# Turning x in 32x32 blocks on VectorE and moving it by transfers, with the token MLP two units later

## The chip, the core and the metric

The kernel runs on one core of one Trainium2 chip. A core has a matrix engine (TensorE), a vector engine (VectorE), an activation engine (ScalarE), a general engine (GpSimd) and a queue engine (SyncE), and 16 DMA engines that move data. Each engine runs its own list of instructions in order and waits on semaphores for the others. The metric is the time of one execution on the device, in microseconds (us); of several runs the median counts.

## The reference: what is computed

An attention with a threshold (only scores within tau of the row's maximum count) is followed by an MLP mixer: a token MLP, which mixes over the sequence, and a channel MLP. There are 8 batch rows, 8 heads, 576 tokens, 64 values a head; all of it is float32.

```python
def _attn_ref(q, k, v, tau):                                   # (8, 8, 576, 64)
    scale = 1.0 / np.sqrt(q.shape[-1])
    scores = scale * np.matmul(q, k.transpose(0, 1, 3, 2))
    thresh = np.max(scores, axis=-1, keepdims=True) - tau
    scores = np.where(scores >= thresh, scores, -1000000000.0)
    scores = scores - np.max(scores, axis=-1, keepdims=True)
    attn = np.exp(scores)
    attn = attn / (np.sum(attn, axis=-1, keepdims=True) + 1e-09)
    return np.matmul(attn, v)

def _moe_ref(x, w_tok1, w_tok2, w_ch1, w_ch2):                 # x: (8, 576, 512)
    xt = x.transpose(0, 2, 1)
    h = np.maximum(xt @ w_tok1, 0.0) @ w_tok2                  # 576 -> 256 -> 576
    u = x + h.transpose(0, 2, 1)
    h2 = np.maximum(u @ w_ch1, 0.0) @ w_ch2                    # 512 -> 1536 -> 512
    return u + h2
```

## The kernel before

The attention is cut into 144 units. A unit is up to 128 queries of two heads, eight or sixteen score matmuls; nine units make two pairs of heads (a half row), 18 make a batch row. In this text rows are counted from 0, as in the code. The unit of the nine whose t is 4 is shared between the two pairs of heads. From row 1 on the weights are turned on VectorE in 32x32 blocks, and 16 transfers per three units put the blocks in their places. SyncE issues them:

```python
    def turn_blocks(u):
        ...
        T = Ts[key]
        nc.vector.transpose(
            out=T[:, :, place, :].rearrange("p a (c x) -> p c a x", c=NK), in_=e.rearrange("p (c a x) -> p c a x", c=NK, a=4)
        )
        if place == GU - 1:                    # GU = 3: the last of three units
            ...
            for a in range(4):
                for i in range(4):
                    nc.sync.dma_start(out=eT[32 * a : 32 * a + 32, :, i, :], in_=T[32 * i : 32 * i + 32, a, :, :])
```

Two units later the values (attention times v) are computed from eT. They come out as x transposed, xT: columns of the model on the partitions, tokens along the row. The token MLP needs x with the tokens on the partitions, so TensorE turns it, and ScalarE copies the result to x_sb:

```python
    def token_mlp(b):
        xT = xTs.pop(b)
        ...
        def turn_x(t):
            M = MT[t]
            ps = ps_tr.tile([P, MAIN], F32, tag="tr", ...).rearrange("p (c x) -> p c x", c=NP)
            for p in range(NP):
                nc.tensor.transpose(out=ps[0:M, p, :], in_=xT[:, p, o + t * P : o + t * P + M], identity=ident)
            nc.scalar.copy(out=x_sb[0:M, t, :], in_=ps[0:M].rearrange("q p d -> q (p d)"))

        def tok1(m):
            ...
            for t in range(NT):
                nc.tensor.matmul(ps, lhsT=w1[:, t, P * m : P * m + P], rhs=x_sb[:, t, :], start=(t == 0), stop=(t == NT - 1))
            nc.scalar.activation(out=s["a"][:, m, :], in_=ps, func=AF.Relu)

        def tok2(c, f):
            ...                                # two matmuls, then xT += result on VectorE

        steps = [(0.44, lambda t=t: turn_x(t)) for t in range(NT)]        # 5 steps of 4 turns
        steps += [(4.3, lambda m=m: tok1(m)) for m in range(NTK)]         # 2 steps
        steps += [(0.97, lambda c=c, f=f: tok2(c, f)) for c in range(NCC) for f in range(2)]   # 8 steps
        return steps
```

The MLP is a list of such steps (the channel MLP gives the others), each with an estimate of its cost. The kernel puts them between the parts of the attention units, a quota in each unit, so that TensorE always has something to do. When the last values of a row are there, its token MLP is put into the list, alternating with old steps of the channel MLP:

```python
    def push(b):
        ...
        for i, step in enumerate(steps):
            n = 2 if i in (NT, NT + NTK) else 1
            todo.extend(old[:n] + [step])
            del old[:n]
        ...
        quota = (sum(c for c, _ in todo) - (KEEP if b else KEEP_FIRST)) / (UB - 1)
```

The end of a unit: ScalarE issues the loads of q and k in most units, and the values that are due are computed last.

```python
        if b_now:
            fill(0.4)
        if back and in_blocks(wb):
            turn_blocks(w)                     # w = u - 2
        ...
        if on:
            weigh(u)                           # the exponentials, with steps of the list between them
        ...
            if t in when:
                ...
                load_qk(n + m, (nc.scalar if b_now else nc.sync,) * 2, range(lo, hi))
        ...
        if due and in_blocks(due[0][1]):
            values_due(u)
```

Of the kernel before, what the change touches and what calls it, by code (L numbers as in the profile page):

```python
# [9 lines left out]
F32 = mybir.dt.float32  # L10
# [3 lines left out]
AF = mybir.ActivationFunctionType  # L14
# [3 lines left out]
P = 128  # L18
# [3 lines left out]
def kernel(  # L22
# [25 lines left out]
    nc = tc.nc  # L48
    B, H, S, D = q.shape
# [7 lines left out]
    NT = NI + 1  # L57
    MT = [P] * NI + [LAST]
    NP = H // 2
    NTK = DTOK // P  # L60
    NCC = DM // P
# [6 lines left out]
    const = ctx.enter_context(tc.tile_pool(name="const", bufs=1))  # L68
    ld = ctx.enter_context(tc.tile_pool(name="ld", bufs=2))
    work = ctx.enter_context(tc.tile_pool(name="work", bufs=2))  # L70
    small = ctx.enter_context(tc.tile_pool(name="small", bufs=6))
    ps_sc = ctx.enter_context(tc.tile_pool(name="ps_sc", bufs=2, space=bass.MemoryType.PSUM))
    ps_tr = ctx.enter_context(tc.tile_pool(name="ps_tr", bufs=2, space=bass.MemoryType.PSUM))

# [9 lines left out]
    units = [(b, 2 * w, t) for b in range(B) for w in range(NP // 2) for t in range(9)]  # L84
# [44 lines left out]
    x_sb = const.tile([P, NT, DM], F32, name="x_sb")  # L129
# [93 lines left out]
    def weight(n):  # L223

        nonlocal steps_done
        for k in range(steps_done, min(steps_done + n, 3 * len(pieces) + 1)):
            i, part = divmod(k, 3)
            if part == 0:
                on_gpsimd(i - 1)
                if i:  # L230
                    load_piece(i - 1 + NRAW)
            else:
                on_scalar(i + 1, part - 1)
            on_vector(i, part)
            steps_done = k + 1

    def weight_to(x):

        weight(max(int(x) - steps_done, 0))

    def need(i):

        weight(3 * i + 4 - steps_done)
# [28 lines left out]
    xTs = {}  # L272
# [3 lines left out]
    def in_blocks(b):  # L276
        return b > 0

    def prep(n):
        lq, lk = loaded.pop(n)  # L280
        made = []
        for src, name in ((lq, "qT"), (lk, "kT")):
            sb = work.tile([P, S], F32, tag=name, name=f"{name}_{n}")
            nc.vector.transpose(out=sb, in_=src.rearrange("p n d -> p (n d)"))  # L284
            made.append(sb)
        heads[n] = made
# [41 lines left out]
    def norm(u):  # L328
        e, rs = st[u]
        rr = small.tile([P, 2], F32, tag="rr", name=f"rr_{u}")  # L330
        nc.vector.tensor_scalar(out=rr, in0=rs, scalar1=1e-9, scalar2=None, op0=ALU.add)
        nc.vector.reciprocal(out=rr, in_=rr)  # L332
        for h in range(2):
            eh = e[:, S * h : S * h + S]
            nc.gpsimd.tensor_scalar(out=eh, in0=eh, scalar1=rr[:, h : h + 1], scalar2=1.0, op0=ALU.mult, op1=ALU.mult)  # L335
        st[u] = e
# [39 lines left out]
    def split_middle(n):  # L376

        lv, vl = vals[n], vlast[n % VL]
        for h in range(2):
            r = slice(D * h, D * h + D)  # L380
            nc.gpsimd.tensor_copy(out=vl[r, r], in_=lv[r, NI, :])
        vals[n] = lv, vl
# [37 lines left out]
                copies.append(lambda x=x, ps=ps: nc.vector.tensor_copy(out=x, in_=ps))  # L420


    def token_mlp(b):
        xT = xTs.pop(b)
        o = S * (b % 2)
        s = {}

        def turn_x(t):
            M = MT[t]
            ps = ps_tr.tile([P, MAIN], F32, tag="tr", name=f"tx_{b}_{t}").rearrange("p (c x) -> p c x", c=NP)  # L430
            for p in range(NP):
                nc.tensor.transpose(out=ps[0:M, p, :], in_=xT[:, p, o + t * P : o + t * P + M], identity=ident)  # L432
            nc.scalar.copy(out=x_sb[0:M, t, :], in_=ps[0:M].rearrange("q p d -> q (p d)"))

        def tok1(m):
            need(2)
            if m == 0:
                s["a"] = work.tile([P, NTK, DM], F32, tag="a", bufs=1, name=f"a_{b}")
            ps = ps_mm.tile([P, DM], F32, tag="mm", name=f"t1_{b}_{m}")
            for t in range(NT):  # L440
                nc.tensor.matmul(ps, lhsT=w1[:, t, P * m : P * m + P], rhs=x_sb[:, t, :], start=(t == 0), stop=(t == NT - 1))  # L441
            nc.scalar.activation(out=s["a"][:, m, :], in_=ps, func=AF.Relu)

        def tok2(c, f):
            need(6)
            ps = ps_mm.tile([P, HS], F32, tag="mm", name=f"t2_{b}_{c}_{f}")
            for m in range(NTK):
                nc.tensor.matmul(  # L448
                    ps, lhsT=s["a"][:, m, P * c : P * c + P], rhs=w2[:, m, HS * f : HS * f + HS], start=(m == 0), stop=(m == NTK - 1)
                )  # L450
            u = xT[:, c, o + HS * f : o + HS * f + HS]
            nc.vector.tensor_add(out=u, in0=u, in1=ps)  # L452

        steps = [(0.44, lambda t=t: turn_x(t)) for t in range(NT)]
        steps += [(4.3, lambda m=m: tok1(m)) for m in range(NTK)]
        steps += [(0.97, lambda c=c, f=f: tok2(c, f)) for c in range(NCC) for f in range(2)]
        return steps
# [49 lines left out]
    def fill(share):  # L507
        nonlocal credit
        credit += share * quota
        while todo and credit > 0:  # L510
            cost, step = todo.popleft()
            credit -= cost
            step()
        if not todo:
            credit = 0.0

    def push(b):
        nonlocal quota
        uT = xTs[b]
        steps, old = token_mlp(b), list(todo)  # L520
        todo.clear()

        for i, step in enumerate(steps):
            n = 2 if i in (NT, NT + NTK) else 1
            todo.extend(old[:n] + [step])
            del old[:n]
        todo.extend(old)
        for i in range(2) if b % 2 == 0 else range(2, (2 * S + GR - 1) // GR):
            todo.extend(channel_mlp(b - b % 2, uT, i))
        quota = (sum(c for c, _ in todo) - (KEEP if b else KEEP_FIRST)) / (UB - 1)  # L530
# [3 lines left out]
    b_now = 0  # L534
    LAG = 2

    def values_due(u):
        while due and due[0][0] <= u:
            _, b, p0, g = due.popleft()
            values(b, p0, g)  # L540
            if p0 == NP - 2 and g == 2:
                if not in_blocks(b):
                    return True
                push(b)
        return False

    for u in range(len(units) + LAG + 4):
        on = u < len(units)
        if u == UB:
            late.close()  # L550
            ps_mm = ctx.enter_context(tc.tile_pool(name="ps_mm", bufs=2, space=bass.MemoryType.PSUM))
        if on:
            b_now, p0, t = units[u]
            n = b_now * NP + p0
        w = u - LAG
        back = 0 <= w < len(units)
        if on:
            scores(u)

        last = False  # L560
        if due and not in_blocks(due[0][1]):
            last = values_due(u)
        if 0 < u <= len(units):
            norm(u - 1)
        if b_now:
            weight(2)
        else:

            weight_to(2.25 * (u - 1.5))
        while copies:  # L570
            copies.popleft()()
        if last:
            push(0)
        if back:
            wb, wp, wt = units[w]
            if not in_blocks(wb):
                for i in range(3):
                    turn(w, i)
            if wt % GU == GU - 1:
                g = wt // GU  # L580
                if g < 2:
                    split_middle(wb * NP + wp + g)
                due.append((u + (2 if in_blocks(wb) else 1), wb, wp, g))
# [3 lines that stand above are left out]
            turn_blocks(w)  # L587
        if b_now:
            weight(2)
        if on:  # L590
            weigh(u)
        elif b_now:
            fill(0.6)
        if b_now:
            weight(2)
        elif u == 0:
            on_scalar(0, 0)
            on_scalar(0, 1)
        else:
            weight_to(2.25 * (u - 1))  # L600
        if on:


            when = {3: (2, 0, 2), 4: (2, 2, 4), 5: (2, 4, 6), 6: (2, 6, 8), 8: (3, 0, 3), 0: (1, 3, 6), 1: (1, 6, 8)}
            if u == 0:
                load_qk(1, (nc.sync, nc.sync), range(0, 3))
            if t in when:
                m, lo, hi = when[t]
                if n + m < len(pairs):
                    load_qk(n + m, (nc.scalar if b_now else nc.sync,) * 2, range(lo, hi))  # L610
            if t in (3, 7) and n + 2 + t // 4 < len(pairs):
                load_v(n + 2 + t // 4)
            if t == 2:
                prep(n + 1)
            if t == 7 and n + 2 < len(pairs):
                prep(n + 2)
        if due and in_blocks(due[0][1]):
            values_due(u)
    need(len(pieces) - 1)
# [30 lines left out]
```

## Time and profile before

| what | before |
|---|---|
| time, median of three | 1379.77 us (1378.82 to 1380.43) |
| span of the profiled execution | 1375.1 us |
| mean granted clock of TensorE | 0.988 |
| the turns of x on TensorE (L432), 160 | 24.0 us busy |
| their copies on ScalarE (L433), 40 | 23.0 us busy, 583 ns each |
| the turns of weights on VectorE (L365), 126 | 172.1 us busy, 1366 ns each |
| the transfers of eT (L374), 672 | 108 KB each, 2.2 us from issue to landing |
| DMA queues of SyncE and ScalarE | 32.0% and 7.3% of the 16 engines' span |

An "L" with a number is a line of the kernel. In a group, "eT<-T" means that eT is written from T; xN counts instructions. "PE" is TensorE, "DVE" VectorE, "ACT" ScalarE, "POOL" GpSimd, "SPq" and "ACTq" the queue instructions of SyncE and ScalarE, among them the issues of transfers. Names: sc scores, e weights, T turned weights, eT moved weights, pv values, tx turned x, t the token MLP, c the channel MLP, g and a their activations. In the trace a float32 matmul of the program counts as two.

### The profile page before, as it was taken

To read this page: it belongs to the slowest core of one execution; us is meant where nothing else is said; L and a number is where in the kernel's file an instruction comes from. 1 tells how busy PE (TensorE), PEld (TensorE's weight loads), DVE (VectorE), ACT (ScalarE), POOL (GpSimd) and SP (SyncE) were. 2 spreads that over 40 slices of the span, in tenths; PEclk is the share of its full clock that TensorE was granted. 3 is DMA by queue.
4 is the path that set the end of the run, shared out by engine and by line. 5 is a ranking of instruction groups with operands and counts; after the bars stand their busy time and mean duration, and the time that the engine had idled before them with its cause. 6 is when DMAs were issued, how large, how long until landed. Compare 5 with 4: busy or idle time off the path is not lost.

```text
span 1375.1 us, 17691 instructions
## 1 busy us (share of the span) xinstructions
PE 1322.7 (96%) x6226; PEld 817.9 (59%) x6226; DVE 588.2 (43%) x1017; ACT 581.8 (42%) x1288; POOL 356.0 (26%) x683
## 2 busy tenths in 40 slices
PE   6877799999999999999999999999999999999998
PEld 3444465646565666565665567565656576575675
DVE  6788875445444443434244444434333453201000
ACT  5666654454445444443434444353333444120110
POOL 4555653222222222222122222222121222100000
PEclk9988999999999999999999999999999999999999
DMA  5434655454544354433344435434433442400000
GB/s 121 98 96 125 183 142 124 100 123 98 122 109 114 82 121 94 113 88 95 77 100 94 113 77 123 106 83 98 103 87 75 107 103 63 115 1 16 8 11 21
DMA packets 278871, 128.20 MB, mean 93 GB/s; under 512 B 200896, under 2 KB 271552, under 8 KB 278784
## 3 DMA queue, kind: packets, MB, share of 16 engines
q1 hardware_dynamic: 150176, 111.06, 32.0%
q10 hardware_dynamic: 128608, 16.01, 7.3%
q8 instruction: 50, 0.82, 0.3%
q14 instruction: 37, 0.30, 0.1%
HBM read 43.25 MB, written 9.44 MB: 38 GB/s over the span
## 4 chain that ended last, share of the span: by engine, by line
PE 85%; DVE 7%; DMA 2%; SPq 2%; ACT 1%; issue 1%; POOL 1%; ACTq 0%; DVEq 0%; POOLq 0%
PE c L486 26%; PE c L470 26%; PE sc L302 11%; PE pv L413 9%; PE t L441 5%; PE t L448 3%; PE pv L408 3%; DVE mx L307 2%; SPq L374 2%; PE tx L432 1%; PE c L482 1%; DMA eT<-T 1%; PE tr L353 1%; DVE wc L205 1%; ACT e L317 1%
## 5 line engine op out<-in xcount | busy, mean ns | idle before, releaser
L307 DVE TENSOR_REDUCE mx<-sc 128x1 f32<-128x576 f32 x288 | 204.5, 751 | 487.9 <-PE sc L302 487.5
L470 PE MATMUL c<-xT,wc 128*128 128x256 f32 (+1 forms) x1920 | 399.4, 362 | 2.1 <-DVE xT L452 1.2
L486 PE MATMUL c<-wc,g 128*128 128x512 f32 x864 | 390.5, 597 | 0.0
L470 PEld LDWEIGHTS c<-xT,wc 128*128 128x128 f32 x1920 | 334.5, 191 | 71.5 <-issue 27.6
L308 POOL TENSOR_SCALAR bias<-mx,toff 128x1 f32<-128x1 f32 x288 | 82.8, 288 | 799.3 <-DVE mx L307 742.3
L317 ACT ACTIVATE e<-sc,bias 128x576 f32<-128x576 f32 x288 | 199.6, 739 | 162.0 <-POOL bias L308 161.4
L486 PEld LDWEIGHTS c<-wc,g 128*128 128x128 f32 x864 | 157.8, 190 | 175.7 <-issue 174.0
L471 ACT ACTIVATE g<-c 128x256 f32<-128x256 f32 (+1 forms) x240 | 86.7, 362 | 334.1 <-PE c L470 317.9
L324 ACT ACTIVATE e<-e,ntau 128x576 f32<-128x576 f32 x288 | 220.7, 771 | 0.0
L335 POOL TENSOR_SCALAR e<-e,rr 128x576 f32<-128x576 f32 x288 | 215.6, 761 | 15.8 <-DVE rr L332 4.3
L302 PE MATMUL sc<-kT,qT 64*128 64x288 f32 (+1 forms) x1280 | 196.6, 447 | 11.1 <-DVE kT L284 7.1
L365 DVE STREAM_TRANSPOSE T<-e 128x1152 f32<-128x1152 f32 x126 | 172.1, 1366 | 6.3 <-DMA eT<-T 2.6
L302 PEld LDWEIGHTS sc<-kT,qT 64*128 64x128 f32 (+1 forms) x1280 | 107.4, 184 | 98.3 <-issue 59.1
L413 PE MATMUL pv<-eT,lv 128*64 128x384 f32 (+1 forms) x1024 | 136.8, 409 | 0.0
L413 PEld LDWEIGHTS pv<-eT,lv 128*64 128x64 f32 x1024 | 76.1, 138 | 51.0 <-issue 43.6
L491 DVE COPY o<-c 128x512 f32<-128x512 f32 x36 | 24.9, 692 | 177.5 <-PE c L486 177.5
L418 ACT COPY xT<-pv 128x384 f32<-128x384 f32 (+1 forms) x56 | 21.0, 401 | 157.5 <-PE pv L413 157.5
L448 PE MATMUL t<-w,a 128*128 128x288 f32 x256 | 75.2, 421 | 7.2 <-DVE xT L452 5.3
L441 PE MATMUL t<-x_sb,w 128*128 128x512 f32 x160 | 72.1, 598 | 0.0
L448 PEld LDWEIGHTS t<-w,a 128*128 128x128 f32 x256 | 45.6, 191 | 32.2 <-issue 11.4
L452 DVE TENSOR_TENSOR xT<-xT,t 128x288 f32<-128x288 f32 x64 | 28.2, 446 | 80.5 <-PE t L448 80.0
L324 ACT ACTIVATION_READ_ACCUMULATOR e<-e,ntau 128x1 f32 x288 | 56.5, 196 | 0.0
(44 smaller groups left out, 554.7 us busy)
## 6 DMA issues: line engine op xcount, KB each, us to landing
eT<-T SPq DMA_DIRECT2D x672, 108.0 KB, 2.2
scratch<-in_moe_w_ch_dram SPq DMA_DIRECT2D x24, 512.0 KB, 3.7
lv<-in_v_dram SPq DMA_DIRECT2D x32, 288.0 KB, 3.3
out_dram<-o SPq DMA_DIRECT2D x36, 256.0 KB, 2.2
lk<-in_k_dram ACTq DMA_DIRECT2D x111, 72.0 KB, 2.6
lq<-in_q_dram ACTq DMA_DIRECT2D x106, 72.0 KB, 2.3
lq<-in_q_dram SPq DMA_DIRECT2D x22, 72.0 KB, 3.2
lk<-in_k_dram SPq DMA_DIRECT2D x17, 72.0 KB, 3.3
```

Source lines behind the costliest of these rows:

```text
L302: nc.tensor.matmul(sc[h][rows, f, 0:HS], lhsT=qT[r, cols], rhs=kT[r, HS * f : HS * f + HS], start=True, stop=True)
L307: nc.vector.tensor_reduce(out=mx[:, c], in_=sc[h][:, :, 0:HS], axis=AX.XY, op=ALU.max)
L317: nc.scalar.activation(out=eh, in_=sc[h][:, :, 0:HS], func=AF.Prelu, bias=bias[:, h : h + 1], scale=SCALE, alpha=STEEP)
L324: nc.scalar.activation(out=eh, in_=eh, func=AF.Exp, bias=ntau, accum_out=rs[:, h : h + 1])
L335: nc.gpsimd.tensor_scalar(out=eh, in0=eh, scalar1=rr[:, h : h + 1], scalar2=1.0, op0=ALU.mult, op1=ALU.mult)
L365: nc.vector.transpose(out=T[:, :, place, :].rearrange("p a (c x) -> p c a x", c=NK), in_=e.rearrange("p (c a x) -> p c a x", c=NK, a=4))
L413: nc.tensor.matmul(to[r], lhsT=lv[:, j, :], rhs=e[j], start=False, stop=(c == NI - 1), skip_group_check=True)
L441: nc.tensor.matmul(ps, lhsT=w1[:, t, P * m : P * m + P], rhs=x_sb[:, t, :], start=(t == 0), stop=(t == NT - 1))
L448: nc.tensor.matmul(ps, lhsT=s["a"][:, m, P * c : P * c + P], rhs=w2[:, m, HS * f : HS * f + HS], start=(m == 0), stop=(m == NTK - 1))
L470: nc.tensor.matmul(ps, lhsT=wc1[:, j, c, :], rhs=uT[:, c, GR * i : GR * i + n], start=(c == 0), stop=(c == NCC - 1))
L471: nc.scalar.activation(out=s["g"][:, j, 0:n], in_=ps, func=AF.Relu)
L486: nc.tensor.matmul(flat, lhsT=s["g"][:, j, P * t : P * t + P], rhs=wc2[:, j, :], start=False, stop=(j == NJ - 1), skip_group_check=True)
```

## The change

From row 2 on x is no longer turned on TensorE. When the values of a half row are there, VectorE turns the half in 32x32 blocks within the next unit, and 16 transfers, half on SyncE and half on ScalarE, put the blocks in their places in x_sb, eight at the end of that unit and eight at the end of the one after. Then, two units later than before, the token MLP is put into the list; it has 10 steps in place of 15. The columns of x_sb stand in another order, so that one transfer moves runs of 64 elements; the activation after tok1 puts them back. The purpose is to free TensorE of the turns and ScalarE of their copies.

```diff
-    small = ctx.enter_context(tc.tile_pool(name="small", bufs=6))
+    small = ctx.enter_context(tc.tile_pool(name="small", bufs=5))
...
+    def x_in_blocks(b):
+        return b > 1
...
+    def turn_x_blocks(b, w):
+        xt = work.tile([P, S // 32 * 64], F32, tag="xt", bufs=1, name=f"xt_{b}_{w}")
+        o = S * (b % 2)
+        nc.vector.transpose(
+            out=xt.rearrange("q (c p d) -> q p c d", c=S // 32, p=2),
+            in_=xTs[b][:, 2 * w : 2 * w + 2, o : o + S].rearrange("q p (c r) -> q p c r", r=32),
+        )
+        return xt.rearrange("q (c x) -> q c x", x=64)
+
+    def move_x(b, w, xt, i):
+        if w == 0 and i == 0:
+            assert x_read[b - 1]
+        for a in range(4):
+            n = len(range(a, S // 32, 4))
+            eng = nc.scalar if a % 2 else nc.sync
+            eng.dma_start(
+                out=x_sb[32 * a : 32 * a + 32, 0:n, P * i + 64 * w : P * i + 64 * w + 64], in_=xt[32 * i : 32 * i + 32, a::4, :]
+            )
...
-            nc.scalar.copy(out=x_sb[0:M, t, :], in_=ps[0:M].rearrange("q p d -> q (p d)"))
+            nc.scalar.copy(out=x_columns(t, M), in_=ps[0:M].rearrange("q p (i d) -> q p i d", i=4))
...
-            nc.scalar.activation(out=s["a"][:, m, :], in_=ps, func=AF.Relu)
+            nc.scalar.activation(
+                out=s["a"][:, m, :].rearrange("q (c i d) -> q i c d", i=4, c=NCC),
+                in_=ps.rearrange("q (i c d) -> q i c d", i=4, c=NCC),
+                func=AF.Relu,
+            )
...
-        steps = [(0.44, lambda t=t: turn_x(t)) for t in range(NT)]
+        steps = [] if x_in_blocks(b) else [(0.44, lambda t=t: turn_x(t)) for t in range(NT)]
...
-            n = 2 if i in (NT, NT + NTK) else 1
+            n = 2 if len(steps) - i in (8, 10) else 1
...
-            if p0 == NP - 2 and g == 2:
+            if g == 2 and x_in_blocks(b):
+
+                moves.append((u, b, p0 // 2))
+            elif p0 == NP - 2 and g == 2:
...
-    for u in range(len(units) + LAG + 4):
+    for u in range(len(units) + LAG + 8):
...
+        if moves and u == moves[0][0] + 1:
+            xts = turn_x_blocks(*moves[0][1:])
...
+        if moves and u > moves[0][0]:
+            at, b, w = moves[0]
+            for i in range(2):
+                move_x(b, w, xts, 2 * (u - at - 1) + i)
+            if u == at + 2:
+                moves.pop()
+                if w:
+                    push(b)
```

The turn on VectorE stands after the maxima and sums of its unit and ahead of the unit's turn of weights; the moves stand after the unit's loads of q and k.

More of the change, by code (lines that the diff above doesn't have):

```diff
@@ L420, in values, with x_columns @@
                 copies.append(lambda x=x, ps=ps: nc.vector.tensor_copy(out=x, in_=ps))
+    x_read = {}
+    def x_in_blocks(b):
+        return b > 1
+    def x_columns(t, M):
+        return x_sb[0:M, t, :].rearrange("q (i p d) -> q p i d", i=4, p=NP)
+    def turn_x_blocks(b, w):
[15 more added lines that the diff above has]
+            )
     def token_mlp(b):
@@ L441, in tok1 @@
                 nc.tensor.matmul(ps, lhsT=w1[:, t, P * m : P * m + P], rhs=x_sb[:, t, :], start=(t == 0), stop=(t == NT - 1))
-            nc.scalar.activation(out=s["a"][:, m, :], in_=ps, func=AF.Relu)
+            nc.scalar.activation(
[3 more added lines that the diff above has]
+            )
+            x_read[b] = m == NTK - 1
         def tok2(c, f):
@@ L535 @@
     LAG = 2
+    moves = []
     def values_due(u):
```

## The prediction

> **What bounds the kernel now.** I read the page's summary and slices first, then the stretches of 100 us, the chain in order of time, the timeline of one unit, the waits. From the page (busy time of each engine; TensorE and its granted clock in 40 slices, in tenths):
>
> ```profile
> PE 1322.7 (96%) x6226; PEld 817.9 (59%) x6226; DVE 588.2 (43%) x1017; ACT 581.8 (42%) x1288; POOL 356.0 (26%) x683
> PE   6877799999999999999999999999999999999998
> PEclk9988999999999999999999999999999999999999
> ```
>
> From about 200 us on TensorE has nothing idle: the stretches view has it busy for 99.2, 97.8, 100.0, 100.0, 100.0, 100.0 us of the six hundreds from 200 to 800. VectorE and ScalarE are under half used there. The change acts only there (it begins with batch row 2, rows counted from 0), so what counts is TensorE time removed, and TensorE time newly spent waiting.
>
> The chain in order of time at row 2 (start, us, what) prices the removed turns:
>
> ```profile
> 428.89 0.44 PE tx L432 x4
> 429.32 2.58 PE c L486 x6
> 431.90 1.17 PE sc L302 x8
> 433.07 0.59 PE tx L432 x4
> ```
>
> A group of four turns takes 0.44 us, 0.59 us just after scores. The channel MLP too takes 2.77 us in place of 2.58 after scores, so that surplus goes to whatever comes next.
>
> The timeline of unit 58, which begins with the scores at 424.91, has what matters most, the SyncE queue:
>
> ```profile
> 427.78 1.36 DVE L365 STREAM_TRANSPOSE T<-e 128x1152 f32<-128x1152 f32 x1
> ...
> 429.21 10.29 SPq L374 DMA_DIRECT2D eT<-T  x16
> ```
>
> VectorE ends the turn of weights 4.2 us into the unit; then SyncE issues the 16 transfers of eT for 10.3 us, 0.60 us each and 0.04 between. The queue is full for more than a unit, though its engine computes nothing. Two lines of the waits (us in total, times, longest), the second from the queue's own list, show how near the edge this is:
>
> ```profile
> PE pv L408 <- DMA eT<-T: 3.3, 4, 1.6
> SPq L374 <- DMA lq<-in_q_dram: 51.8, 22, 4.8
> ```
>
> The first: TensorE already waits for eT now and then. The second: an eT transfer waits for a q load that ScalarE issues. No data ties the two. The built program counts the landing of all these transfers on eight counters, used in turn by both queues, and an issue waits until the counter's last user has landed.
>
> **What the Trainium skill says.** The page "VectorE: DVE Perf Modes", section "The three transpose paths": VectorE turns only 32x32 blocks within a bank, TensorE a whole 128x128 into PSUM. Hence the extra transfers here. Its times are for bf16; the trace's are used. "DMA: Bandwidth & Descriptors", section "Issuing engines are not separate DMA queues": transfers from all engines share the same DMA engines, and issuing from two only saves issue time, usually small. The trace disagrees on small: 10.29 us a burst. The same page, "Anatomy of one DMA — SWDGE (gpsimd) path", gives about 2 us of fixed cost for that path; eT on SyncE's queue lands 2.2 us after issue here. "TensorE: Matmul & The Clock Gate", section "Why this matters for your kernels": idle gaps over some 3 us between bursts halve the clock. The trace agrees: the clock is 0.91 in the two hundreds up to 200 us, where TensorE's timeline has gaps of 2 to 3.6 us (3.59 at 114.4), and 1.00 after.
>
> **The change part by part.**
>
> *Removed.* 30 groups of four turns (6 rows by 5). At row 2 they take 3 x 0.44 + 2 x 0.59 = 2.50 us, less 2 x 0.15 that passes on: 2.2 to 2.5 a row, **13 to 15 us** in all, every one of them on the path. Also 30 ScalarE copies of 583 ns, 17.5 us, beside other work: nothing.
>
> *Added on VectorE.* 12 turns of 128x1152, at 1366 ns (the weights' turn of the same size) 16.4 us, beside other work. But each stands ahead of the turn of weights in the unit after the values, so that unit's eT burst begins 1.4 us later: 5.7 us into the unit.
>
> *Added transfers.* 16 for each half row, half on each queue, eight in each of two units. In SyncE's order all eight of its moves come after the 16 of eT. At 0.35 to 0.6 us each (the range of SyncE's other issues in the trace: output 0.36, v 0.40 to 0.53, eT 0.60) with an output between, they take 4 to 5.5 us of queue.
>
> *Moved.* The token MLP stands two units later and two old steps ahead of its first matmul. I laid the changed kernel's TensorE order out with the durations of the chain (scores 1.17, 1.13 in the shared unit; two steps of second channel layer 5.35; one 2.77; a step of first layer 1.79, two after scores 3.65; values 3.38), from the start of the unit after the values:
> - rows 3 and 5: (1.13 + 5.35) + (1.17 + 2.77 + 1.79) + (1.17 + 3.65) = **17.0 us** until tok1.
> - row 2: 6.5 + 7.0 + 9.9 + 1.2 = 24.6 us; rows 4 and 6: 8.4 + 8.7 + 9.9 + 1.2 = 28.2 us. Values stand between here.
> - row 7: no scores are left and no burst stands in the way; 18 us for a chain of some 10.
>
> When is x there? Counters aside: 5.7 + 10.3 + 4 to 5.5 + 2.2 = 22 to 24 us. With the counters: in rows 3 and 5 the thirteenth eT issue waits for ScalarE's k load of the next unit to land, and the first and third moves of SyncE for ScalarE's own moves. Unit 59's second exponential ends 6.3 us after its scores in the trace; the next unit begins at 6.5, so 12.8, plus about 1 us because ScalarE itself waits for the landings of its q and k loads before two of its moves, load issues 0.8 and landing 2.5 (page: 2.6 for k): about 17. Four more eT issues, 2.6, then 5 of moves and output, then 2.2: about **26 us**. So tok1 of rows 3 and 5 waits between 5 (no counters) and 9 us; I take 7.5, **15 us for two**. A gap of that length also costs clock: one stretch of 3.4 us at half speed, as the clock record shows them in the first 200 us, 1.7 us each, **3 us**.
>
> The same counters push the end of eT itself in the eleven units that hold moves and a burst: the last issue ends at 18.9 to 19.6 us and lands 2.2 later, at 21 to 22 us (20 in unit 49, which is short). By the same laying out the values that need it come, in units 49, 58, 67, 85, 94, 103, 121, 130, 139, at 17.3, 19.9, 19.2, 24.2, 23.7, 21.1, 24.2, 23.7, 21.1 us (76 and 112 hold the waits of tok1 counted above). They fall short by some 2.7, 1.5, 2.5, 0, 0, 0.5, 0, 0, 0.5: **about 7 us at full; I take 4**, because today's waits for eT (3.3) fall partly at the same places.
>
> *No weight.* The columns of x stand in another order, which the activation after tok1 undoes by its output pattern; 16 activations of 597 ns on ScalarE, not on the path. Buffers of the small tiles go from six to five, which makes room for the turned x; none lives five units.
>
> Sum: -14 + 15 + 3 + 4 = +8. I shade it to +4, since every wait in it is an estimate that stacks the later of several times: **1384 us**.
>
> **Rivals.**
> 1. *Hidden transfers*: x arrives in time, only the removal counts: 1379.8 - 14 = 1366. For it: two units of extra delay were put in for just this, DMA engines are busy only 40 to 50% in the stretches, and rows 2, 4, 6, 7 come out in time. Against: SyncE's queue order in rows 3 and 5, which even without counters gives 22 us against 17.0.
> 2. *A wait takes the removal's place* (mine): 1375 if only the queue order counts (-14 + 2 x 5), 1388 with counters.
> 3. *ScalarE blocks*: its moves wait for eT transfers issued late in the burst, its exponentials slip, score buffers stay occupied, and TensorE waits for ScalarE in every moving unit: 11 x 2 to 4 us more, 1400 to 1420. Against: in the built order ScalarE's moves mostly wait for early ones of the burst or its own loads, and its engine is 42% busy.
> 4. *VectorE the bound*: 16.4 us on an engine used 40 of 100 us; worth nothing here.
>
> **Range and chances.** 2% is 27.6 us. Faster by that would take twice the removed turns: 0.02. Slower by that needs rival 3: 0.05. Within 2%: 0.93. The range that holds 8 in 10 goes from most of rival 1 (1367) to my sum with waits at full and some of rival 3: 1396.
>
> **What would show it.** TensorE: turns x160 become x40, busy less by 15 to 18 us; VectorE gains 12 turns of about 1.37 us. The waits get a new line, tok1 on the move of x, two long waits (5 to 10 us) in units 78 and 114 and none in rows 4, 6 and 7. The wait of values on eT grows from 3.3 to 6 to 12. SyncE's bursts of eT in moving units last 13 us or more. The clock dips after the two gaps. I am wrong if the tok1 wait is absent (then 1366), if it shows in even rows, or if TensorE waits for the weights' activation in ScalarE (rival 3).

## The result and the profile after

The changed kernel takes **1399.83 us** (median of 5 runs, 1399.02 to 1403.59) against 1379.77 before: 1.0147 times the time before, 95% interval 1.0127 to 1.0167. It is 20 us slower. The prediction was 1384.0 with a range of 1367 to 1396; the result lies above the range.

The page of the changed kernel, its summary and slices:

```profile
PE 1316.8 (94%) x6106; PEld 808.8 (58%) x6106; DVE 603.6 (43%) x1029; ACT 565.1 (40%) x1258; POOL 355.9 (25%) x683
PE   6877899999999999799999999979999999999998
PEclk8988999999999999999999999989999999999999
```

TensorE has 120 instructions less (6226 to 6106), but only 5.9 us less of busy time (1322.7 to 1316.8), and the span is 21.8 us longer. Past its first five slices the row of PE now has two 7s, the 17th slice (559 to 594 us) and the 27th. Up to the scores of unit 30 (211.28 us before, 213.35 after) TensorE has the same work; the traces of this text reach them at 210.9 to 216.8 us, so two traces can differ by some us there. From these scores to TensorE's last instruction it takes 1160.0 us before and 1179.7 after, and of this its idle time rises from 5.7 to 30.5 us. The waits of the changed kernel name it (us in total, times, longest):

```profile
PE t L471 <- DMA x_sb<-xt: 18.7, 3, 8.9
PE sc L302 <- ACT e L317: 9.2, 7, 2.0
PE pv L408 <- DMA eT<-T: 2.8, 3, 1.7
```

The first line is new: tok1 (tile t) waits for the transfers of x. The three waits are 8.89 us at 584.9 (unit 78, row 3), 8.56 us at 913.8 (unit 114, row 5) and 1.26 us at 1232.2 (row 7). Before, the second line read

```profile
PE sc L302 <- ACT e L317: 3.9, 4, 1.9
```

with all four waits in the first 200 us; now 3.96 us of the 9.2 lie after them. The wait of values for eT was 3.3 us and is not larger now.

The timeline of unit 76, whose scores stand in the chain at 567.89, shows how the first long wait arises (start, us, queue or engine, what, how many):

```profile
570.69 1.36 DVE L436 STREAM_TRANSPOSE xt<-xT 128x1152 f32<-128x1152 f32 x1
...
573.38 12.89 SPq L374 DMA_DIRECT2D eT<-T  x16
...
586.32 2.55 SPq L448 DMA_DIRECT2D x_sb<-xt  x4
588.98 0.53 SPq L527 DMA_DIRECT2D out_dram<-o  x1
589.55 2.54 SPq L448 DMA_DIRECT2D x_sb<-xt  x4
...
593.76 6.97 PE L471 MATMUL t<-x_sb,w 128*128 128x512 f32 x10 [8.89 <-DMA x_sb<-xt]
```

VectorE has x turned by 572.05, 4.2 us into the unit. SyncE takes up its eight moves only at 586.32, behind the 16 transfers of eT (12.89 us), and spends 5.77 us on them and an output. The last of them lands at 593.4, 25.5 us into the unit and 1.9 us after its own issue, so it is the issue that is late and not the transfer; the matmuls begin at 593.76. TensorE had reached tok1 at 584.87, 17.0 us into the unit.

The stretch ahead of the slow clock and the slow one (duration, then busy time of each engine, PEclk, share of DMA engines, GB/s):

```profile
578.00:588.40 10.40, 6.86 (x33) 4.98 (x31) 4.91 (x7) 4.84 (x12) 2.90 (x6) 1.00 0.64 151
588.40:598.60 10.20, 4.84 (x6) 2.19 (x7) 0.00 (x0) 0.00 (x0) 0.00 (x0) 0.50 0.16 48
```

The clock stands at 0.50 for 10.2 us. The first 5.4 us of it pass in the wait itself; the other 4.84 us are matmuls at half speed, which cost 2.4 us. The same happens once more at 916.1. The matmuls of tok1 take 66.0 us after 200 us in place of 61.4.

The chain of the changed kernel at row 2, where no tok1 waits, has a wait of the other kind:

```profile
452.29 4.50 PE t L471 x10
...
456.82 0.60 ACT a L472
457.42 0.64 ACT e L317
...
458.10 1.86 PE sc L302 x8
```

Before, a step of the channel MLP stood between the scores and tok1 there, and the scores behind tok1 did not wait:

```profile
451.58 2.77 PE c L486 x6
454.36 4.29 PE t L441 x10
458.65 1.17 PE sc L302 x8
```

In the changed kernel tok1 is the first step after the scores in this unit, and the only one. Its activation (a) stands ahead of the unit's exponentials (e) on ScalarE, and can't start before tok1 ends; so the exponentials start late, the score buffers come free late, and the next scores wait 1.32 us and then take 1.86 us in place of 1.17. That happens once in each of the rows 2, 4 and 6 (456.8, 778.1, 1106.2).

### The profile page after: what moved, and what is told of

It is laid out like the page before. It is cut to its first block, busy times and chain, and to the rows that moved or that the text cites. A ratio compares the mean times of both kernels' runs of the same rounds, so it can differ in the third digit from the quotient of the medians.

```text
span 1396.9 us, 17642 instructions
## 1 busy us (share of the span) xinstructions
PE 1316.8 (94%) x6106; PEld 808.8 (58%) x6106; DVE 603.6 (43%) x1029; ACT 565.1 (40%) x1258; POOL 355.9 (25%) x683
## 4 chain that ended last, share of the span: by engine, by line
PE 83%; DVE 7%; DMA 3%; SPq 2%; ACT 2%; issue 1%; POOL 1%; ACTq 0%; DVEq 0%; POOLq 0%
PE c L521 26%; PE c L505 25%; PE sc L302 11%; PE pv L413 8%; PE t L471 5%; PE t L483 4%; PE pv L408 3%; DVE mx L307 3%; SPq L374 2%; PE c L517 1%; DMA lk<-in_k_dram 1%; DVE wc L205 1%; ACT e L317 1%; PE tr L353 1%; DMA scratch<-in_moe_w_ch_dram 1%
## 5 line engine op out<-in xcount | busy, mean ns | idle before, releaser
L471 PE MATMUL t<-x_sb,w 128*128 128x512 f32 x160 | 76.5, 627 | 18.7 <-DMA x_sb<-xt 18.7
L471 PEld LDWEIGHTS t<-x_sb,w 128*128 128x128 f32 x160 | 31.3, 201 | 56.7 <-issue 54.4
```

## The experiments

All ratios are to the kernel before, run beside the experiment on the same chip. Line numbers shift by a few between variants. "Idle" means TensorE's idle time from the scores of unit 30 to its last instruction: 5.7 us before, 30.5 us in the changed kernel. "In the trace" times are of that same part, in one profiled execution each.

### Without the transfers of x

```diff
-            for i in range(2):
-                move_x(b, w, xts, 2 * (u - at - 1) + i)
```

From row 2 on, x_sb is not written any more, so the token MLP takes row 1's x in every later row. TensorE's order is that of the changed kernel.

> The changed kernel without its transfers of x (rows 2 to 7 then take row 1's x into the token MLP); every instruction of TensorE stands as in the changed kernel. My theory (the loss is waiting for the moved x, its clock cost and ScalarE held up by its moves): no wait of tok1 on the moves, no half clock after 200 us, so 1399.8 less 18.7 less 5 less 4, about 1372 us (1368 to 1377), that is the removed turns as a clear gain of some 8 us. Rival A (the new order of work, two units later and with ten steps, is what costs): TensorE's waits move elsewhere and it stays above 1390 us.

1375.22 us, 0.9963 (0.9953 to 0.9973). The group line of tok1:

```profile
L471 PE MATMUL t<-x_sb,w 128*128 128x512 f32 x160 | 71.8, 595 | 0.0
```

No wait, and no matmul at half clock. So the transfers cost 1399.83 - 1375.22 = 24.6 us (25.4 by the two ratios). But removing the turns and paying for no transfer saves only 5 us, and not the 14 us that the turns took (their busy time after 200 us falls from 16.7 to 2.6). Idle is 10.8 us, 5.2 more than before: scores 4.0 (0 before), channel MLP waiting for xT 2.2 (0.2), values 2.2 (2.4) and the second token layer 2.2 (2.8).

### The order alone, with the turns kept

```diff
-        steps = [] if x_in_blocks(b) else [(0.44, lambda t=t: turn_x(t)) for t in range(NT)]
+        steps = [(0.0 if x_in_blocks(b) else 0.44, lambda t=t: turn_x(t)) for t in range(NT)]
 ...
+            if x_in_blocks(b) and i < NT:
+                if i == 2:
+                    todo.append(old.pop(0))
+                todo.append(step)
+                continue
```

The turns and moves of x are taken out, and the turns on TensorE put back into the changed kernel's order, two and three groups around one old step.

> The changed kernel's order, but x turned by TensorE as before: the token MLP joins the list two units later, no turn by VectorE and no transfer of x, and the five groups of four turns of a row stand two and three around the old step ahead of its first matmul. Otherwise the order on TensorE is that of the changed kernel. Leaving the transfers out (turns gone, order changed) saved only 5 us of the 14 us of turns. My theory is that the order itself costs the rest: then this kernel, with turns and with that order, is 6 to 10 us slower than the kernel before: 1386 to 1390 us, with 1.3 us waits of scores for ScalarE in the even rows as in the changed kernel. The rival: the turns are worth only some 5 us because what they take comes back elsewhere, whatever the order; then it takes the time of the kernel before, 1379 to 1382 us.

1389.35 us, 1.0064 (1.0050 to 1.0078): 8.8 us slower than before, inside what the order theory expected; the rival falls. The chain of this kernel at row 2 has the same wait of scores behind tok1's activation:

```profile
451.55 4.50 PE t L471 x10
...
456.07 0.60 ACT a L472
456.67 0.64 ACT e L317
...
457.35 1.87 PE sc L302 x8
```

Idle is 12.5 us: scores 4.0, channel MLP waiting for xT 1.8, and 3.7 ahead of the turns themselves, which here stand close together and wait for ScalarE to empty their two buffers (0.2 before). Those 3.4 us more belong to how I placed the turns; the changed kernel does not have them. So by the medians the order accounts for 8.8 - 3.4 = 5.4 us of the 9 us missing from the turns' price.

The traces go further: 1160.0 us before, 1172.0 here, 1154.8 without the transfers. In the same order, then, leaving the turns out gives 17.2 us, 3.4 of them those waits and 13.8 the turns' own, which is their price in full. The order costs 12.0 - 3.4 = 8.6 us, and about 1.7 of these come from a stretch of 3.4 us at half clock (at 773.9) that the kernel without transfers does not have. In both kernels scores wait 4.0 us and are busy 1.9 us longer than before. So the order is most of the 9 us; whether it is all of it stays open.

### The transfers, three ways

**Token MLP three units later.**

```diff
-            if u == at + 2:
+            if u == at + 3:
                 moves.pop()
```

(The moves stay in the first two units.)

> The token MLP joins the list three units later in place of two, all else as in the changed kernel. My theory: x is there 25.9 us after the start of its moving unit, as in the trace, and tok1 of rows 3 and 5 now stands at 27 to 30 us: the two waits of 8.9 and 8.6 us and the two stretches at half clock vanish, the small waits of scores stay: 1375 to 1381 us. Rival A (lateness itself costs): later is worse, 1400 us or more. Rival B (DMA engines too slow for the moves): waits of tok1 shrink but stay, 1385 to 1395 us.

1376.24 us, 0.9967 (0.9954 to 0.9980). No tok1 wait; about 1 us from the kernel without transfers, though not in the same order: scores wait for ScalarE once and not three times, and values wait 4.8 us in place of 2.2. One unit more takes the moves out of tok1's way, not out of that of the values.

**The turn of x behind the turn of weights**, so that the burst of eT starts 1.4 us earlier:

```diff
-        if moves and u == moves[0][0] + 1:
-            xts = turn_x_blocks(*moves[0][1:])
 ...
             turn_blocks(w)
+        if moves and u == moves[0][0] + 1:
+            xts = turn_x_blocks(*moves[0][1:])
```

> VectorE turns x after its unit's weights, not ahead of them; TensorE's order is the same. The burst of eT then begins 1.3 us earlier. My theory: x still stands behind the whole burst, and the burst still waits for ScalarE's k load of the next unit, so tok1's waits shrink by 0 to 1.3 us each: 1397 to 1400 us. Rival C (the turn ahead of the weights is what makes x and eT late): the waits shrink by most of their length, below 1390 us.

1398.34 us, 1.0126 (1.0093 to 1.0158). The tok1 waits are 8.19, 8.09 and 1.26: shorter by 0.7 and 0.5. VectorE's turn counts on this path, for less than its length.

**ScalarE's moves all in the first unit, and its q and k loads in other units**, so that nothing of SyncE's burst waits for a load:

```diff
-            when = {3: (2, 0, 2), 4: (2, 2, 4), 5: (2, 4, 6), 6: (2, 6, 8), ...}
+            when = {3: (2, 0, 4), 6: (2, 4, 8), ...}
 ...
-            for i in range(2):
-                move_x(b, w, xts, 2 * (u - at - 1) + i)
+            first = u == at + 1
+            for i in range(4):
+                move_x(b, w, xts, i, ((1,) if first else ()) + ((0,) if first == (i < 2) else ()))
```

> ScalarE issues all eight of its moves at the end of the first unit and none in the second, and the four loads of q and k of the two moving units go to the units beside them, so that no eT transfer shares a counter with a later ScalarE transfer; SyncE's queue and TensorE's order are the same. My theory (the queue order is most of it, the counters some): the burst of eT falls from 12.9 to 10.3 us, and tok1 of rows 3 and 5 waits 6 to 7 us in place of 8.6 and 8.9: 1393 to 1397 us. Rival D (the shared counters are all of it): no wait, 1378 us. Rival E (counters have no part): burst and waits unchanged, 1400 us.

1401.97 us, 1.0145 (1.0115 to 1.0176): the time missed what was expected. The burst took 11.16 us (12.89 in the changed kernel, 10.3 expected) and the waits 6.96 and 7.18, close to what was expected; so of the 9 us the coupling of SyncE's issues to ScalarE's is worth 1.4 to 1.9, and most of the rest is queue. Waits of values rose from 3.2 to 4.0 and of scores from 4.0 to 4.6, and ScalarE's exponentials waited up to 5.3 us for landings of x. Idle fell by only 2.2 us, to 28.3, and the interval is wider than that; whether a small gain is there stays open.

### SyncE's moves ahead of its burst

```diff
+            for i in range(4):
+                move_x(*moves[0][1:], xts, i, 0)        # SyncE's, right behind the turn of x
 ...
-                move_x(b, w, xts, 2 * (u - at - 1) + i)
+                move_x(b, w, xts, 2 * (u - at - 1) + i, 1)      # ScalarE's alone
```

> The changed kernel, but SyncE issues all eight of its moves of x in the unit after the values, ahead of that unit's burst of eT, in place of two in that unit and the next. The order on TensorE is the same. My theory is that time on SyncE's queue is what lacks: then the two waits of tok1 fall from 8.9 and 8.6 to some 1 us each, but the burst begins about 5 us later, eT lands at some 23 us, and by the laid-out order the values then wait in units 49 (5.9), 58 (3.3), 67 (4), 103 and 139 (2.1 each): 15 to 20 us of waits of values for eT, and 1393 to 1397 us in all. The rival, that only the place of the moves behind the burst costs: tok1 waits gone and values as before, some 1378.

1406.42 us, 1.0185 (1.0152 to 1.0217): slower still. The waits of this kernel:

```profile
PE pv L408 <- DMA eT<-T: 11.3, 5, 5.5
...
PE t L473 <- DMA x_sb<-xt: 1.0, 1, 1.0
```

and its timeline around unit 49:

```profile
372.05 10.50 SPq L374 DMA_DIRECT2D eT<-T  x16
...
384.72 1.55 PE L408 MATMUL pv<-eT,vl 128*64 128x384 f32 x4 [5.52 <-DMA eT<-T]
```

The two long waits of tok1 are gone (1.78 and 1.67 us are left in their places, and 1.02 in row 7; the page puts 1.8 down to ScalarE). In their stead the burst starts later and TensorE waits 19.5 us ahead of values, the page putting 11.3 of that down to eT. Idle is 32.6 us, no less than with the moves behind the burst. So what lacks is time on SyncE's queue before TensorE needs the data; which of the two transfers goes first only chooses who waits. The places were laid out well: 5.9, 3.3 and 4 us were expected in units 49, 58 and 67, and 5.52, 2.86 and 4.33 came; 1.29 and 1.96 in units 103 and 139, and 1.11 and 1.46 in two where none was expected. The time came out 9 us above the expectation. The clock is part of that: after 200 us it is at half for 6.8 us once and 3.4 us three times. No run used fewer issues or another queue, so that either would do is not shown.

### Some rows only

`x_in_blocks(b)` as `b in (2, 4, 6, 7)`:

> Only rows 2, 4, 6 and 7 take x by turns on VectorE and transfers; rows 3 and 5 are turned on TensorE as before. The list of work shifts with that: laid out with the trace's durations, tok1 stands 24.6 (row 2), 21.7 (row 4) and 20.8 us (row 6) after the start of the moving unit. My theory (tok1 waits exactly where it stands ahead of the arrival of x, at 26 to 28 us): no wait to speak of in row 2, 4 to 6 us in rows 4 and 6, which had none in the changed kernel, and no wait in rows 3 and 5; 1383 to 1391 us. Rival (something about rows 3 and 5 themselves): no waits at all, 1368 to 1374 us.

1400.35 us, 1.0136 (1.0111 to 1.0161): missed by 9 us. Rows 4 and 6, which did not wait in the changed kernel, wait 5.01 and 3.45 us (4 to 6 expected), so it is the place of tok1 and not the row that decides. Row 7 again waits 1.24, and waits of values grow to 8.5 us. With the turns kept in the rows between, other steps fall into other units, and the slack of a row moves with them.

`x_in_blocks(b)` as `b in (3, 5)`:

> Only rows 3 and 5 take x by transfers. Laid out, tok1 stands 20.1 us after the start of the moving unit in both, 3 us later than in the changed kernel. My theory: x arrives at 26 us in row 3 and some 1.5 us later in row 5, whose moving unit is longer, so waits of 5 to 7 us each in place of 8.9 and 8.6, still with stretches at half clock: 1380 less 5 plus 12 plus 4, about 1391 us (1387 to 1394). Rival (the waits depend on the rows, not on where tok1 stands): 8.9 and 8.6 again, 1397 us.

1389.67 us, 1.0062 (1.0041 to 1.0084), as expected. The waits of tok1 are 6.08 and 5.83 us, with the clock at half for 6.8 us after each. The two parts cost 8.6 and 18.8 us (ratio times 1382.12), 27 in all, where both together cost 20: the rows don't add up, since each sets where the next one's steps fall.

`return False` (the smaller pool and the code alone):

> The changed kernel with no row by transfers: what stays of the change is the small pool with five buffers, the other order of the columns of x in the copies and in the activation after tok1, and the longer loop. My theory: these cost nothing, 1378 to 1382 us, a ratio of 1.000. Rival (they cost the 2 us that the profile of the changed kernel is behind by at 150 us): 1382 us or more, a ratio of at least 1.0015.

1380.1 us, 0.9990 (0.9978 to 1.0002): what is not moved of x costs nothing.

### Both mends, and beyond

**Three units later and the turn of x behind the turn of weights:**

> Both: the token MLP three units later, and VectorE's turn of x after the unit's turn of weights, so that eT is 1.3 us earlier in the units that move x. My theory: no waits of tok1, and the waits of values on eT (4.8 us in the run three units later) fall to 1 to 2: 1372 to 1376 us. Rival (x and eT share the DMA engines, and that sets the waits of values): 1376 us as without it.

1374.74 us, **0.9947 (0.9932 to 0.9963)**: the lowest ratio here, 7.4 us faster than before on the same chip. That the second mend adds to the first is not shown: the intervals overlap, and in the trace the two variants take 1154.1 and 1153.8 us. The waits for transfers that are left:

```profile
PE pv L408 <- DMA eT<-T: 2.4, 2, 1.9
PE pv L408 <- DMA x_sb<-xt: 1.7, 1, 1.7
```

Values wait 4.2 us in all, and not 1 to 2 as expected. Idle is 9.4 us. The 1.32 us wait of scores for ScalarE comes once (464.5), not three times: in rows 4 and 6 it is absent, as with three units alone.

**The same with row 1 too** (`b > 0`):

> The variant with the token MLP three units later and the turn of x behind the turn of weights, with row 1 of the batch also moved by transfers. If a row's turns on TensorE are worth what a row of that variant gained (7.4 us for six rows, 1.2 a row, up to the 2.3 of turns removed): 1371 to 1374 us, 1 to 2 us below it. Rival: VectorE and the queues still carry the loading and turning of token weights up to about 200 us, then row 1's tok1 waits some us and the gain is gone: 1375 to 1380.

1383.01 us, 1.0016 (1.0004 to 1.0029): slower than without, by more than the rival had it (the profiled execution took 1378.2). No tok1 waits; scores and values do, in the timeline while row 1's x is moved:

```profile
291.73 11.29 SPq L374 DMA_DIRECT2D eT<-T  x16
...
293.91 1.24 PE L302 MATMUL sc<-kT,qT 64*128 64x288 f32 x8
...
297.20 2.66 PE L302 MATMUL sc<-kT,qT 64*128 64x288 f32 x8 [2.05 <-ACT e L317]
...
305.28 1.55 PE L408 MATMUL pv<-eT,vl 128*64 128x384 f32 x4 [5.42 <-DMA lq<-in_q_dram]
```

The wait is put down to a q load, but the last eT transfer was issued at 303.0 and the values start 2.3 us after it, so by time it is eT. The clock is then at half for 10.2 us. TensorE was at these values 8.1 us after the burst began, sooner than a burst alone takes. The reason is not the one the rival gave: SyncE's moves of x in this unit begin at 303.73, behind the last eT. Between the scores at 293.91 and the values TensorE has no step of the MLP at all, where the variant without row 1 has turns of x and tok1. The list had run empty: row 0 leaves only 20 us of work in hand (KEEP_FIRST), the later rows 45, and row 1's token MLP came three units later. No run raised KEEP_FIRST, so this is read from the trace and the code, not tested.

**The same with more work in hand** (`KEEP = 51.0` in place of 45.0):

> The variant with the token MLP three units later and the turn of x behind the turn of weights, with the amount of work kept in hand for TensorE raised from 45 to 51. By the laid-out order the values of units 49, 58 and 67 then come 16.5 to 20 us into their units, earlier than eT lands (20 to 22): waits of values for eT grow from 4.2 to 8 to 12, while waits of scores fall by some 2: 1376 to 1382 us. Rival: the amount in hand is what limits, 1370 to 1373.

1376.84 us, 0.9967 (0.9953 to 0.9981): in the expected range, but not for the expected reason. Waits of values came to 4.9 us and not to 8 to 12, and those of scores stayed at 1.3. Beside 0.9947 (0.9932 to 0.9963) with 45 no gain shows, and the rival falls.

## Why the prediction was wrong, point by point

| step of the prediction | predicted, us | measured, us |
|---|---|---|
| turns removed, "every one of them on the path" | -14 | their busy time -14.1; the time only -5 without transfers |
| two waits of tok1 | 15 | 17.4 (8.89 + 8.56) |
| row 7 | 0 | 1.3 |
| half clock | 3 | 4.6 |
| waits of values for eT | 4 | 1 (2.2 without transfers, 3.2 with them) |
| what the new order costs | not in the sum | 9 |
| sum | 8, shaded to 4 | 19 to 20 |

The right-hand sum is -14.1 + 17.4 + 1.3 + 4.6 + 1 + 9 = 19.2, beside 20.1 measured.

**What held.** The mechanism and its places: two long waits in units 78 and 114, none in rows 2, 4 and 6. Tok1 was reached at 17.0 us, as laid out. That x was there at "about 26 us" (25.9 to the first matmul) is in part luck: the terms of that sum (17, 2.6, 5, 2.2) make 26.8, and the burst's last issue ended 18.4 us into the unit and not at 19.6. Turns fell from 160 to 40, VectorE made 12 turns of 1358 ns (12 of about 1.37 us predicted), the burst in unit 76 took 12.9 us (13 or more predicted), and the clock dipped after the two gaps. Rival 1, the hidden transfer, was wrong: with three units of delay tok1 no longer waits, but 1376.24 came and not 1366. Rival 3, ScalarE blocking TensorE in every moving unit, did not come. The sign named for it did, "TensorE waits for the weights' activation in ScalarE", three times 1.32 us; but these waits are there without any transfer too.

**What else missed.** TensorE was to be busy 15 to 18 us less and is 5.9 less, above all since tok1 and the scores take longer. The wait of values for eT was to grow to 6 to 12 us and is 2.8. Of the six hundreds read as the start, the last is busy for 99.1 us and not 100.0, which changes nothing.

**The step that failed most** is the sum: it takes the turns as removed, "every one of them on the path", and has no term for the new order, which it used only to find where tok1 and the values fall. The price of the turns was right (13.8 us in the same order). But that order puts tok1 alone behind the scores in rows 2, 4 and 6, where its activation holds up the exponentials, and puts channel steps close behind the additions that they read. Without any transfer only 5 us of the 14 are gained, so 9 us are missing; with the turns kept, the order by itself costs 5.4 us by the medians and 8.6 in the trace. The layout had the durations for it: tok1 4.3 us, then 0.6 for the activation and 0.64 for an exponential, against a next pair of scores due as soon as tok1 ends.

**"I take 7.5"** failed as a compromise. The layout with counters gave 26 - 17.0 = 9, and 9 is what came; 5 was the answer for a program without those counters, which wasn't the one to be run. The same holds for "I shade it to +4": the terms were not too high but too few.

**"One stretch of 3.4 us at half speed"** was mis-sized: the stretches last 10.2 us, about half of them inside the wait, so each cost 2.3 us and not 1.7. The stretches of 3.4 us in the first 200 us came after gaps of 2.2 to 3.0 us, not after one of nearly 9, and the same 200 us also hold one of 6.8 and one of 13.7. The Trainium skill, "TensorE: Matmul & The Clock Gate", section "Why this matters for your kernels", puts the threshold at some 3 us of idle time. The traces here have stretches at half clock after gaps of 1.3 to 3.0 us too, so it does not hold as a limit for this kernel.

**The waits of values** were set at 4 and are 1. In the places where less than 3 us were missing by the layout, 1.6 us came in unit 49 and little in the others; where more was missing, as with SyncE's moves ahead of the burst, the layout was right within 0.5 us. Its error is of the size of the small ones.

**Issue time.** The page "DMA: Bandwidth & Descriptors", section "Issuing engines are not separate DMA queues", says that a second issuer saves only issue time, usually small beside the transfer itself. One issue is small here too, 0.60 us beside 1.9 us (x) and 2.3 us (eT) to landing. But they add up on one queue: 16 transfers of eT and eight moves take 18.7 us of SyncE, with an output and some 2.6 us of waiting among them, and the two long waits hang on that, while the DMA engines are busy for 0.64 of the stretch.

## What to carry to other kernels

An engine that only issues transfers has a timetable as full as a computing one: count its instructions times their issue time, and put their consumer behind the sum; here one unit more turned 20 us of loss into 4 us of gain. A removed instruction on the bounding engine gives its whole time back only if the order that replaces it has no new waits, so lay the whole new order out, the consumers of every shared engine included, and not only the wait one has in mind. When the layout gives a number, take it; halving it between two cases of which only one is built is no estimate.

## What was not expected of the hardware

- Moves of x cost the queue the same as the larger transfers of eT: 0.602 us median on SyncE and 0.617 on ScalarE for 40 KB, 0.60 for the 108 KB of eT. Between these two sizes the issuer spends the same time.
- After 200 us, the half-speed stretch lengthens with the gap: none or 3.4 us after gaps of 1.3 to 4.3, 6.8 after ones of 5.0 to 7.0, 10.2 after ones of 7.2 to 8.9. It starts 2 to 5.3 us after the gap began (588.4 for the gap from 584.9). One stretch stands outside this: 10.2 us in the kernel with row 1, which began at 298.1, behind a gap of 2.05 and ahead of one of 5.42. And in the first 200 us, where gaps follow each other closely, the kernel before has 6.8 us after a gap of 2.2; so the length of one gap alone does not settle it.
- A matmul of tok1 took 1192 ns in such a stretch in place of 592, so what is left of a dip at the end of the wait falls on whatever stands behind it.
